# Matmuls of the identity behind the first sums and scores, and the sums' second half moved behind the first scores

## The chip, the cores and the metric

The kernel runs on one core of a Trainium2 chip. The metric is device time in microseconds of one execution. A core has TensorE (PE in the profile; PEld is its loading of weights), VectorE (DVE), ScalarE (ACT), GpSimd (POOL) and SyncE (SP, which here issues the DMAs).

## What is computed

Three layers over 4 sequences of 576 positions. The change lies in the first, attention with 8 heads of 64 per sequence, so 32 heads, handled as 16 pairs:

```python
def _attn_ref(q, k, v, s) -> np.ndarray:
    B, H, S, D = q.shape
    scale = 1.0 / np.sqrt(D)
    scores = scale * np.matmul(q, k.transpose(0, 1, 3, 2))
    causal = np.triu(np.ones((S, S), dtype=bool), k=1)
    s_pos = np.maximum(s, 0.0)
    cum = np.cumsum(s_pos, axis=-1)
    bias = -(cum[:, :, :, None] - cum[:, :, None, :])
    scores = np.where(causal, -1000000000.0, scores + np.minimum(bias, 0.0))
    scores = scores - np.max(scores, axis=-1, keepdims=True)
    attn = np.exp(scores)
    attn = attn / (np.sum(attn, axis=-1, keepdims=True) + 1e-09)
    return np.matmul(attn, v).astype(np.float32)
```

Behind it come a gated feed-forward layer with a mixing over positions, and a layer that mixes positions with weights turned by the sine and cosine of a projection.

## The kernel before

Values in 32 bits are multiplied as a high and a low part, three matmuls for one product. The order of an engine's instructions is worked out ahead of the run by a scheduler with a timeline of its own, from priorities and data dependences; `issue_after(x)` puts an instruction behind x on its engine, and `high_priority` puts it ahead of what else is ready. On the chip each engine works through its list in that order.

**The start.** `run` (L899) makes the identity on GpSimd, loads s, and loads Q and K of pair 0 (`load_pair`, L261). `cumulate` (L183) then makes the running sums of s for all 32 heads: 12 matmuls against triangles of ones into two tiles `cumo` (32 rows), copied to `ch` on ScalarE and to `cpos` on VectorE, with `cl` the rest; `cpos` goes to DRAM (`cd`), from where `load_cum` (L272) fetches the sums of later pairs, spread over 128 rows, by DMA. For pair 0 the spread is done by 8 matmuls with a selecting matrix `sel` into two tiles `cumb`, copied to `C` by ScalarE (L231). `split_pair` (L289) makes qh, ql, kh and kl of a pair on ScalarE, GpSimd and VectorE. Q and K have one buffer each, so a load of K waits for the split kl of the pair before; the four parts and E have two buffers.

**The scores.** `score_units` (L305) works in two groups per pair, for both heads at once on the two halves of the array's rows: the first has tiles t = 4, 1 and 0, the second t = 3 and 2. Each product is three pairs of matmuls, and the causal mask is added by pairs of bf16 matmuls (`mpick`, `mlow`). All matmuls of a group are put one behind the other by `row` (L108) into one tile `sc` of four PSUM banks, of which there is one. VectorE then adds C and takes the extremum of each row (L344), which frees the tile for the next group; ScalarE takes the exponential (L350).

**The step.** `attention` (L461) goes through 17 steps by the string `ORDER`: in step p come the two score groups of pair p ("s"), the transposes of pair p-1 ("t", `transpose_units` L357, with ScalarE or VectorE copying each bank to `Ef` or `E0`), the product with v of pair p-2 ("v", `pv_units`), the loads and splits of pair p+1 ("p") and conversions of the feed-forward weights ("c", `convert`, whose pieces `PLAN` deals out). Some transposes use the pool `psT` of two banks, and in the first four pairs others use `psF`. From step 5 on the feed-forward layer's matmuls are dealt in between as filling; the first steps have none.

**PSUM** has eight banks. `psS` (the scores, four) and `psT` (two) lie on the right, `psF` (two) on the left; the four banks of `cumulate` lie on the left and are given back before `psF` is made.

Of the kernel before, what the change touches and what calls it, by code (L numbers as in the profile page):

```python
# [9 lines left out]
F32 = mybir.dt.float32  # L10
F32R = mybir.dt.float32r
U32 = mybir.dt.uint32
BF16 = mybir.dt.bfloat16
# [3 lines left out]
PSUM = bass.MemoryType.PSUM  # L17
DRAM = bass.MemoryType.DRAM

B, H, S, D = 4, 8, 576, 64  # L20
DM, DFF = 512, 1024
FH = DFF // 2
P = 128
# [14 lines left out]
HALF = [(0, 288), (288, 288)]  # L38
# [15 lines left out]
class Kernel:  # L54
# [50 lines left out]
    def mm(self, out, lhsT, rhs, start, stop):  # L105
        return self.nc.tensor.matmul(out, lhsT, rhs, start=start, stop=stop)  # L106

    def row(self, calls):  # L108


        before = None
        for c in calls:
            with ExitStack() as es:
                if before is not None:
                    es.enter_context(self.tc.high_priority())
                    es.enter_context(self.tc.issue_after(before.ins))
                before = self.mm(*c)


    def pace(self, ns):  # L120
# [62 lines left out]
    def cumulate(self, es):  # L183
        nc = self.nc
        p, sT = self.cum, self.sT
        ps = self.pool(es, "cumps", space=PSUM)
        self.cpos = cpos = p.tile([32, S], F32, name="cpos")


        tri = p.tile([P, 832], F32R, name="tri")  # L190
        neg = p.tile([P, 544], F32R, name="neg")
        sh = p.tile([P, 5, 32], F32R, name="sh")
        sl = p.tile([P, 5, 32], F32R, name="sl")
        trif = p.tile([P, P], F32, name="trif")
        nc.gpsimd.memset(trif, 1.0)
        nc.gpsimd.affine_select(
            out=trif, in_=trif, pattern=[[1, P]], compare_op=ALU.is_ge, fill=0.0, base=0, channel_multiplier=-1
        )
        nc.vector.memset(f32(tri[:, 0:512]), 0.0)
        nc.vector.memset(f32(tri[:, 512 + P:]), 1.0)  # L200
        nc.vector.tensor_copy(tri[:, 512:512 + P], trif)
        nc.vector.memset(f32(neg[:, 0:256]), -1.0)
        nc.vector.memset(f32(neg[:, 256 + P:]), 0.0)
        nc.vector.tensor_scalar(neg[:, 256:256 + P], trif, -1.0, None, op0=ALU.add)
        nc.vector.tensor_scalar(sT, sT, 0.0, None, op0=ALU.max)
        nc.vector.tensor_copy(sh, sT)
        nc.vector.tensor_tensor(sl, sT, f32(sh), op=ALU.subtract)
        ch = p.tile([32, S], F32R, name="ch")
        cl = p.tile([32, S], F32R, name="cl")
        sel = p.tile([32, 2, P], F32R, name="sel")  # L210
        nc.vector.tensor_copy(sel, self.ident[0:32, 0:2].unsqueeze(2).to_broadcast([32, 2, P]))
        self.cums[0] = self.a1.tile([P, 2, S], F32, name="C", tag="C", bufs=2)
        for a, n in HALF:
            o = ps.tile([P, 512], F32, name="cumo", tag=f"cumo{a}")
            tiles = ((0, neg, 256), (1, neg, 128), (2, tri, 256)) if a == 0 else (
                (2, tri, 544), (3, tri, 416), (4, tri, 288))
            for i, (t, w, c) in enumerate(tiles):
                for part in (sh, sl):
                    self.mm(o[0:32, 0:n], part[:, t, :], w[:, c:c + n],
                            i == 0 and part is sh, i == 2 and part is sl)  # L220
            cs = slice(a, a + n)
            nc.scalar.copy(ch[:, cs], o[0:32, 0:n])
            nc.vector.tensor_copy(cpos[:, cs], o[0:32, 0:n])
            nc.sync.dma_start(self.cd[:, cs], cpos[:, cs])
            nc.vector.tensor_tensor(cl[:, cs], cpos[:, cs], f32(ch[:, cs]), op=ALU.subtract)

            for j in (0, 1):
                o = ps.tile([P, 512], F32, name="cumb", tag="cumb", bufs=2)
                self.mm(o[:, 0:n], sel[:, j], ch[:, cs], True, False)
                self.mm(o[:, 0:n], sel[:, j], cl[:, cs], False, True)  # L230
                nc.scalar.copy(self.cums[0][:, j, cs], o[:, 0:n])  # L231

    def attention_pools(self, es):
        nc = self.nc
# [20 lines left out]
            self.nc.vector.memset(r, 0.0)  # L255

    def attention_psum(self, es):
        self.psS = self.pool(es, "psS", side="right", space=PSUM)
        self.psT = self.pool(es, "psT", bufs=2, side="right", space=PSUM)

    def load_pair(self, pr):  # L261
# [43 lines left out]
    def score_units(self, pr):  # L305

        nc = self.nc
        qh, ql, kh, kl = self.ops.pop(pr)
        C = self.cums.pop(pr)
# [5 lines left out]
        for group in GROUPS:  # L315
            calls, sums, cost = [], [], 0.0
            four = self.psS.tile([P, 2, 2, 512], F32, name="sc", tag="sc")
            for i, bank in enumerate(group):
                o = four[:, i]
                for t, a, n, col in bank:  # L320
# [13 lines left out]
                    if a == 0:  # L334
                        sums.append((t, four[:, :, :, 0:n] if t == 4 else four[:, i:i + 1, :, col:col + n]))
                    cost += 3 * max(107.0, w / 2.4) + 120 * len(masks) + 120
            self.row(calls)
            for t, o in sums:
                c = (t - 1) % 5
                n = QE[t]  # L340
# [120 lines left out]
    def attention(self):  # L461
        n = B * H // 2
        for p in range(n + 1):
            su = self.score_units(p) if p < n else iter(())
            tu = self.transpose_units(p - 1) if p > 0 else iter(())

            v = p > 1 and (p - 2) % 4 != 3
            pv = self.pv_units(p - 2) if v else iter(())
            for o in self.ORDER_V if v else self.ORDER:
                if o == "r":  # L470
                    if p > 0:
                        self.load_r(p - 1)
                    continue
                if o == "c":
                    self.convert(p)
                    continue
                if o == "p":
                    if p + 1 < n:
                        self.load_cum(p + 1)
                        self.split_pair(p + 1)  # L480
                    if p + 2 < n:
                        self.load_pair(p + 2)
                    if p < n - 1:
                        with self.tc.issue_after(self.summed[p + 1].ins):
                            self.load_v(p)
                    elif p < n:
                        self.load_v(p)
                    continue
                c = next({"s": su, "t": tu, "v": pv}[o], None)
                self.mark()  # L490
                if c is not None:
                    self.pace(c)
            self.run_units([tu])
            if p > 0 and p % 4 == 0:
                self.run_units([self.pv_units(p - 1)])
                b = p // 4 - 1
                if b < B - 1:
                    self.drain()
                    self.fill = self.ffn(b)
# [399 lines left out]
    def run(self):  # L899
        nc = self.nc  # L900
        with ExitStack() as root, ExitStack() as right2, ExitStack() as left2:
# [9 lines left out]
            self.ident = self.cp.tile([P, P], F32, name="ident")  # L911
            make_identity(nc, self.ident)
            self.attention_pools(att)
            self.load_s(cs)
            self.load_pair(0)
            with self.tc.high_priority():
# [2 lines left out]
            self.load_pair(1)  # L919
            self.constants()  # L920
            self.fill_aux()
            cs.close()
            self.f1 = self.pool(left, "f1")
            self.f2 = self.pool(left, "f2", bufs=2)
# [1 line left out]
            self.f3 = self.pool(f3s, "f3")  # L926
            self.in_done, self.ratio = True, self.RATIO_IN
            self.ffn_weights()
            psl = ExitStack()
            self.psF = self.pool(psl, "psF", bufs=2, side="left", space=PSUM)  # L930
            self.ftags, self.turn = ("fo",), 0
            with ExitStack() as aps:
                self.attention_psum(aps)
                self.attention()
            att.close()
# [131 lines left out]
```

## Time and profile before

| What | Value |
|---|---|
| Median of 3 runs | 674.57 us (673.63 to 678.18) |
| Profiled execution | 674.18 us, of which the span is 672.3 us |
| TensorE busy | 634.8 us, 94% of the span, 4676 matmuls |
| Weight loads (PEld) | 556.9 us, 83% |
| VectorE busy | 427.4 us, 64% |
| ScalarE busy | 363.2 us, 54% |
| GpSimd busy | 179.0 us, 27% |
| DMA | 83.57 MB, mean 124 GB/s |
| TensorE, 0 to 80 us | 65.19 of 80 us |
| TensorE, 80 to 420 us | 320.94 of 340 us |

A share of busy time is a mean over stages with different limits; the stage that the change touches is the first 60 us or so. Matmuls of one engine are pipelined, so the printed durations of neighbours overlap, and the distance between two starts is the better measure of what one costs. The granted clock is given as a share of full speed: 1.00 is 2.4 GHz, 0.50 is 1.2 GHz, and a value between the two means a change of level inside the stretch.

### The profile page before, as it was taken

How to read it: one execution, taken by the hardware profiler on the slowest of the kernel's cores; microseconds unless marked ns; L12 is line 12 of the kernel's file. 1: busy time of each engine (PE TensorE's matmuls, PEld its weight loads, DVE VectorE, ACT ScalarE, POOL GpSimd, SP SyncE). 2: the span in 40 equal slices, each digit the busy share in tenths (PEclk: the TensorE clock that was granted, in tenths of full speed). 3: DMA queues.
4: the chain of work that ended last, by engine and by line, in shares of the span. 5: the costliest groups of instructions: out<-in, count | busy, mean ns of one | idle time of the engine just before them, and what ended most of it. 6: DMA issues, size and time to landing. Idle time of an engine off the chain costs nothing.

```text
span 672.3 us, 12581 instructions
## 1 busy us (share of the span) xinstructions
PE 634.8 (94%) x4676; PEld 556.9 (83%) x4676; DVE 427.4 (64%) x1048; ACT 363.2 (54%) x836; POOL 179.0 (27%) x203
## 2 busy tenths in 40 slices
PE   5889989989999999999997888999999999999997
PEld 4666667778777888778787788898999999989997
DVE  5578856765567563773259977887773477458412
ACT  3767768774688844775155435565550454245100
POOL 4234532433314423044397633220000100100000
PEclk9989999999999999999999889999999999999999
DMA  4556753266632565201355879831001200300101
GB/s 145 190 182 215 233 163 120 77 191 207 203 104 74 169 190 185 73 31 63 119 144 162 266 244 356 264 109 61 1 1 70 73 0 36 106 1 1 71 1 71
DMA packets 50189, 83.57 MB, mean 124 GB/s; under 512 B 8432, under 2 KB 20176, under 8 KB 50128
## 3 DMA queue, kind: packets, MB, share of 16 engines
q1 hardware_dynamic: 50128, 82.76, 38.4%
q8 instruction: 37, 0.61, 0.4%
q14 instruction: 24, 0.20, 0.1%
HBM read 61.61 MB, written 21.13 MB: 123 GB/s over the span
## 4 chain that ended last, share of the span: by engine, by line
PE 65%; ACT 10%; DMA 8%; DVE 8%; POOL 4%; issue 4%; SPq 1%; DVEq 0%; ACTq 0%; POOLq 0%
PE yo L106 17%; PE fo L106 13%; PE th L106 8%; PE co L106 8%; PE wo L106 6%; PE Y L106 4%; PE sc L106 4%; PE T L375 4%; ACT E L350 3%; POOL vT L653 2%; DMA wraw<-in_moe_w_tok_i 1%; PE tp L802 1%; DMA wraw<-in_moe_w_tok_r 1%; DMA wraw<-wd 1%; ACT vT L701 1%
## 5 line engine op out<-in xcount | busy, mean ns | idle before, releaser
L350 ACT ACTIVATE E<-E,negm 128x576 f32<-128x576 f32 (+4 forms) x160 | 92.8, 587 | 2.3 <-DVE negm L344 2.1
L106 PE MATMUL yo<-wkh,zh 128*128 128x288 f32 x288 | 85.3, 296 | 0.2 <-DVE x2T L875 0.2
L106 PE MATMUL yo<-wkl,zh 128*128 128x288 f32 x288 | 85.2, 296 | 0.0
L106 PE MATMUL yo<-wkh,zl 128*128 128x288 f32 x288 | 85.2, 297 | 0.0
L344 DVE CUSTOM_DVE_ANT_0 E<-sc,C 128x576 f32<-128x576 f32 (+4 forms) x160 | 68.2, 486 | 13.5 <-PE sc L106 11.3
L375 PE MATMUL T<-ident,E 128*128 128x128 f32 x400 | 64.2, 292 | 11.1 <-ACT Ef L383 5.6
L375 PEld LDWEIGHTS T<-ident,E 128*128 128x128 f32 x400 | 54.0, 193 | 17.1 <-ACT Ef L383 8.8
L106 PE MATMUL fo<-x,wih 128*128 128x288 f32 x256 | 56.0, 304 | 1.4 <-ACT uT L721 1.4
L106 PEld LDWEIGHTS yo<-wkh,zh 128*128 128x128 f32 x288 | 54.1, 188 | 0.7 <-DVE x2T L875 0.4
L106 PEld LDWEIGHTS yo<-wkl,zh 128*128 128x128 f32 x288 | 54.1, 188 | 0.3
L106 PEld LDWEIGHTS yo<-wkh,zl 128*128 128x128 f32 x288 | 54.0, 188 | 0.1
L106 PE MATMUL co<-u,wch 128*128 128x288 f32 x256 | 53.0, 295 | 0.0
L99 POOL TENSOR_SCALAR xt<-x2s 128x128 fp32r<-128x128 f32 x16 | 10.8, 688 | 155.8 <-DVE x2s L103 155.8
L106 PE MATMUL wo<-gh,woh 128*128 128x288 f32 x128 | 39.3, 310 | 8.1 <-ACT gh L95 4.7
L106 PEld LDWEIGHTS fo<-x,wih 128*128 128x128 f32 x256 | 41.8, 188 | 4.0 <-ACT uT L721 2.2
L106 PE MATMUL fo<-wih,x 128*128 128x512 f32 x128 | 43.3, 404 | 1.3 <-ACT x L95 0.7
L387 DVE COPY Ef<-T 128x512 f32<-128x512 f32 x32 | 21.8, 684 | 34.9 <-PE T L375 31.5
L106 PE MATMUL th<-wth,x2s 128*128 128x512 f32 x128 | 42.9, 400 | 0.0
L95 ACT CAST u<-x2T 128x576 fp32r<-128x576 f32 x16 | 10.7, 672 | 59.3 <-DVE x2T L875 59.3
L106 PE MATMUL sc<-kl,qh 64*128 64x288 f32 (+1 forms) x192 | 39.0, 397 | 3.0 <-DVE negm L344 3.0
L106 PEld LDWEIGHTS co<-u,wch 128*128 128x128 f32 x256 | 41.7, 188 | 0.0
L297 POOL TENSOR_TENSOR kl<-K,kh 128x576 fp32r<-128x576 f32 x15 | 21.8, 1452 | 67.2 <-ACT kh L95 36.9
(193 smaller groups left out, 1775.7 us busy)
## 6 DMA issues: line engine op xcount, KB each, us to landing
C<-cd SPq DMA_DIRECT2D x15, 576.0 KB, 6.1
Q<-in_q SPq DMA_DIRECT2D x16, 288.0 KB, 3.8
K<-in_k SPq DMA_DIRECT2D x16, 288.0 KB, 3.9
xT<-rd SPq DMA_DIRECT2D x32, 144.0 KB, 2.9
xd<-xT SPq DMA_DIRECT2D x16, 288.0 KB
gd<-uT SPq DMA_DIRECT2D x16, 288.0 KB, 4.4
gr<-gd SPq DMA_DIRECT2D x16, 288.0 KB
xr<-xd SPq DMA_DIRECT2D x16, 288.0 KB, 3.5
```

What stands on the lines that cost most here:

```text
L95: nc.scalar.copy(out, src)
L99: nc.gpsimd.tensor_scalar(out, src, 1.0, 1.0, op0=ALU.mult, op1=ALU.mult)
L106: return self.nc.tensor.matmul(out, lhsT, rhs, start=start, stop=stop)
L297: low = nc.gpsimd.tensor_tensor(kl, K, f32(kh), op=ALU.subtract)
L344: nc.vector.tensor_tensor_reduce(at.rearrange("p (i n) -> p i n", i=m), o[:, :, j], C[:, j, 0:n].rearrange("p (i n) -> p i n", i=m), -1.0, ...
L350: nc.scalar.activation(at, at, AF.Exp, bias=negm[:, j, c:c + 1], scale=-1.0, accum_out=sm[:, j * 5 + c:j * 5 + c + 1])
L375: nc.tensor.transpose(T[:, col:col + P], e, self.ident)
L387: nc.vector.tensor_copy(Ef[:, 512:1024], T)
L653: nc.gpsimd.tensor_scalar(vT[0:r, t], vT[0:r, t], rs[0:r, t:t + 1], nm[0:r, t:t + 1], op0=ALU.mult, op1=ALU.add)
L701: nc.scalar.activation(vT, vT, AF.Gelu_apprx_tanh)
L802: nc.tensor.transpose(tp[0:r, dt * P:(dt + 1) * P], x2T[:, dt, a:a + r], self.ident)
```

## The change

A new method `spin` issues n matmuls of the identity, read as 256 columns of bf16, into a PSUM tile that nothing reads. Each is put behind the one before it, at high priority. There are spins at three kinds of places: 14 at the head of `cumulate`; 20 behind the sums' second half in pair 0, into a tile `spun` that takes a bank of `cumo`; and 12 behind the second score group of pairs 0, 1 and 2, into a bank of `psT`.

The 8 matmuls that spread the first pair's sums, and their ScalarE copies, become a function `spread`, which `score_units` calls for pair 0 behind the last matmul of the first score group. For that, the first group of pair 0 is generated before `cumulate`'s pools are given back, `psS` is opened ahead of `cumulate`, and `attention` takes up the generator that has been started. `row` now returns its last matmul.

```diff
--- before.py
+++ after.py
@@ -105,6 +105,18 @@
     def mm(self, out, lhsT, rhs, start, stop):
         return self.nc.tensor.matmul(out, lhsT, rhs, start=start, stop=stop)
 
+    def spin(self, o, n, before=None):
+
+
+        one = self.ident.bitcast(BF16)
+        for _ in range(n):
+            with ExitStack() as es:
+                if before is not None:
+                    es.enter_context(self.tc.issue_after(before.ins))
+                    es.enter_context(self.tc.high_priority())
+                before = self.mm(o[:, 0:256], one[:, 0:P], one, True, True)
+        return before
+
     def row(self, calls):
 
 
@@ -115,6 +127,7 @@
                     es.enter_context(self.tc.high_priority())
                     es.enter_context(self.tc.issue_after(before.ins))
                 before = self.mm(*c)
+        return before
 
 
     def pace(self, ns):
@@ -185,6 +198,23 @@
         p, sT = self.cum, self.sT
         ps = self.pool(es, "cumps", space=PSUM)
         self.cpos = cpos = p.tile([32, S], F32, name="cpos")
+        o = ps.tile([P, 512], F32, name="spin", tag="cumb", bufs=2)
+        self.spin(o, 14)
+        self.spun = ps.tile([P, 512], F32, name="spun", tag="cumo0")
+
+        def spread(before):
+
+            for a, n in HALF:
+                cs = slice(a, a + n)
+                for j in (0, 1):
+                    o = ps.tile([P, 512], F32, name="cumb", tag="cumb", bufs=2)
+                    with self.tc.issue_after(before.ins):
+                        self.mm(o[:, 0:n], sel[:, j], ch[:, cs], True, False)
+                        last = self.mm(o[:, 0:n], sel[:, j], cl[:, cs], False, True)
+                    nc.scalar.copy(C[:, j, cs], o[:, 0:n])
+            return last
+
+        self.spread = spread
 
 
         tri = p.tile([P, 832], F32R, name="tri")
@@ -209,7 +239,7 @@
         cl = p.tile([32, S], F32R, name="cl")
         sel = p.tile([32, 2, P], F32R, name="sel")
         nc.vector.tensor_copy(sel, self.ident[0:32, 0:2].unsqueeze(2).to_broadcast([32, 2, P]))
-        self.cums[0] = self.a1.tile([P, 2, S], F32, name="C", tag="C", bufs=2)
+        C = self.cums[0] = self.a1.tile([P, 2, S], F32, name="C", tag="C", bufs=2)
         for a, n in HALF:
             o = ps.tile([P, 512], F32, name="cumo", tag=f"cumo{a}")
             tiles = ((0, neg, 256), (1, neg, 128), (2, tri, 256)) if a == 0 else (
@@ -224,12 +254,6 @@
             nc.sync.dma_start(self.cd[:, cs], cpos[:, cs])
             nc.vector.tensor_tensor(cl[:, cs], cpos[:, cs], f32(ch[:, cs]), op=ALU.subtract)
 
-            for j in (0, 1):
-                o = ps.tile([P, 512], F32, name="cumb", tag="cumb", bufs=2)
-                self.mm(o[:, 0:n], sel[:, j], ch[:, cs], True, False)
-                self.mm(o[:, 0:n], sel[:, j], cl[:, cs], False, True)
-                nc.scalar.copy(self.cums[0][:, j, cs], o[:, 0:n])
-
     def attention_pools(self, es):
         nc = self.nc
         side = "right"
@@ -255,7 +279,6 @@
             self.nc.vector.memset(r, 0.0)
 
     def attention_psum(self, es):
-        self.psS = self.pool(es, "psS", side="right", space=PSUM)
         self.psT = self.pool(es, "psT", bufs=2, side="right", space=PSUM)
 
     def load_pair(self, pr):
@@ -334,7 +357,11 @@
                     if a == 0:
                         sums.append((t, four[:, :, :, 0:n] if t == 4 else four[:, i:i + 1, :, col:col + n]))
                     cost += 3 * max(107.0, w / 2.4) + 120 * len(masks) + 120
-            self.row(calls)
+            last = self.row(calls)
+            if pr < 3 and group is GROUPS[-1]:
+                self.spin(self.psT.tile([P, 512], F32, name="spin", tag="T"), 12, last)
+            elif pr == 0:
+                self.spin(self.spun, 20, self.spread(last))
             for t, o in sums:
                 c = (t - 1) % 5
                 n = QE[t]
@@ -461,7 +488,7 @@
     def attention(self):
         n = B * H // 2
         for p in range(n + 1):
-            su = self.score_units(p) if p < n else iter(())
+            su = self.first if p == 0 else self.score_units(p) if p < n else iter(())
             tu = self.transpose_units(p - 1) if p > 0 else iter(())
 
             v = p > 1 and (p - 2) % 4 != 3
@@ -486,7 +513,10 @@
                     elif p < n:
                         self.load_v(p)
                     continue
-                c = next({"s": su, "t": tu, "v": pv}[o], None)
+                if p == 0 and o == "s" and self.lead:
+                    c, self.lead = self.lead, None
+                else:
+                    c = next({"s": su, "t": tu, "v": pv}[o], None)
                 self.mark()
                 if c is not None:
                     self.pace(c)
@@ -911,6 +941,9 @@
             self.ident = self.cp.tile([P, P], F32, name="ident")
             make_identity(nc, self.ident)
             self.attention_pools(att)
+            psl = ExitStack()
+            aps = ExitStack()
+            self.psS = self.pool(aps, "psS", side="right", space=PSUM)
             self.load_s(cs)
             self.load_pair(0)
             with self.tc.high_priority():
@@ -919,6 +952,8 @@
             self.load_pair(1)
             self.constants()
             self.fill_aux()
+            self.first = self.score_units(0)
+            self.lead = next(self.first)
             cs.close()
             self.f1 = self.pool(left, "f1")
             self.f2 = self.pool(left, "f2", bufs=2)
@@ -926,10 +961,9 @@
             self.f3 = self.pool(f3s, "f3")
             self.in_done, self.ratio = True, self.RATIO_IN
             self.ffn_weights()
-            psl = ExitStack()
             self.psF = self.pool(psl, "psF", bufs=2, side="left", space=PSUM)
             self.ftags, self.turn = ("fo",), 0
-            with ExitStack() as aps:
+            with aps:
                 self.attention_psum(aps)
                 self.attention()
             att.close()
```

## Rows read from the trace of the kernel before

**Rows 1.** Busy by stretch: PE, PEld, DVE, ACT, POOL; clock, DMA share, GB/s.

```profile
0.00:80.00 80.00, 65.19 (x515) 48.45 (x517) 55.70 (x173) 52.76 (x152) 32.05 (x43) 0.94 0.59 184
80.00:420.00 340.00, 320.94 (x2448) 271.31 (x2445) 219.40 (x593) 207.90 (x507) 134.70 (x144) 0.99 0.50 159
```

**Rows 2.** TensorE's timeline, pair 0: start us, us, what, count, [idle, releaser].

```profile
4.30 0.45 PE L106 MATMUL cumo<-neg,sh 128*32 128x288 f32 x1 [4.30 <-DVE sh L206]
...
7.18 0.44 PE L106 MATMUL cumo<-tri,sl 128*32 128x288 f32 x1
...
8.73 0.44 PE L106 MATMUL sc<-kh,ql 64*128 64x288 f32 x2
8.97 0.44 PE L106 MATMUL sc<-kh,qh 64*128 64x288 f32 x2
...
9.80 0.44 PE L106 MATMUL sc<-mpick,mlow 64*128 64x128 bf16 x4
10.00 0.59 PE L106 MATMUL sc<-kl,qh 64*128 64x288 f32 x2
...
13.99 0.44 PE L106 MATMUL cumb<-cl,sel 32*128 32x288 f32 x1
```

**Rows 3.** TensorE's timeline, pairs 1, 2 and 4.

```profile
21.96 0.61 PE L106 MATMUL sc<-kl,qh 64*128 64x288 f32 x2
...
25.38 0.33 PE L106 MATMUL sc<-mpick,mlow 64*128 64x128 bf16 x2
...
28.10 0.47 PE L106 MATMUL sc<-kl,qh 64*128 64x448 f32 x2 [0.17 <-DVE negm L344]
...
29.44 0.29 PE L106 MATMUL sc<-mpick,mlow 64*128 64x128 bf16 x4
...
32.79 0.70 PE L375 MATMUL T<-ident,E 128*128 128x128 f32 x2 [1.24 <-ACT E L350]
33.42 0.61 PE L106 MATMUL sc<-kl,qh 64*128 64x288 f32 x2
...
47.15 0.49 PE L375 MATMUL T<-ident,E 128*128 128x128 f32 x1 [2.44 <-ACT Ef L383]
...
63.19 0.40 PE L106 MATMUL sc<-kl,qh 64*128 64x288 f32 x2
...
65.05 0.23 PE L106 MATMUL sc<-mpick,mlow 64*128 64x128 bf16 x2
```

**Rows 4.** Busy in half microseconds, columns as in rows 1.

```profile
32.50:33.00 0.50, 0.21 (x1) 0.21 (x2) 0.00 (x0) 0.50 (x3) 0.50 (x1) 0.93 0.78 281
...
36.00:36.50 0.50, 0.50 (x12) 0.50 (x10) 0.00 (x0) 0.00 (x0) 0.00 (x0) 0.66 0.89 370
46.50:47.00 0.50, 0.00 (x0) 0.00 (x0) 0.50 (x3) 0.50 (x3) 0.50 (x1) 0.58 0.07 8
```

**Rows 5.** Chain of waits, in order of time: start us, us, what.

```profile
7.81 3.14 DMA K<-in_k
...
13.79 0.76 DVE ql L300
...
16.90 2.89 PE sc L106 x20
...
22.30 3.44 DMA C<-cd
...
32.05 0.70 ACT E L350 x2
...
33.49 3.35 PE sc L106 x27
...
44.18 1.79 DVE wtab L510
...
51.91 0.74 DVE E L344
```

**Rows 6.** GpSimd's timeline: the identity.

```profile
2.16 0.30 POOL masks.py:199 TENSOR_SCALAR_AFFINE_SELECT ident<-ident 128x128 f32<-128x128 f32 x1
```

## The prediction

> **What bounds the kernel now.** I read the busy time by stretch first [rows 1]. From 80 us on, TensorE is busy 320.94 of 340 us, so 94%: there the order of TensorE's work sets the time, and the change adds nothing to it. In the first 80 us it is busy 65.19 us, so some 15 us are waits. A microsecond won there reaches the end, because everything later starts that much sooner; a microsecond won on TensorE where another engine is late is lost again.
>
> The second view is TensorE's timeline of the first pair of heads [rows 2]. The two matmuls of a score pair run side by side, and pairs of 288 columns start 0.24 us apart (8.73, 8.97): 288 / 0.24 = 1.2 columns per ns, the lower of the clock's levels, 1.2 GHz. That stands although the clock column prints 0.94 as the mean of the first 80 us; the reader is to go by the starts here. The same groups later show the other level [rows 3]: the first score group of a pair takes 21.96 to 25.38 + 0.33 = 25.71, 3.75 us, in pair 1, and 63.19 to 65.05 + 0.23 = 65.28, 2.09 us, in pair 4. The second group takes 2.89 us from 16.90 in pair 0 [rows 5] and 28.10 to 29.44 + 0.29 = 29.73, 1.63 us, in pair 1. The prices of the low level are thus 3.75 - 2.09 = 1.66 us for a first group and 2.89 - 1.63 = 1.26 us for a second.
>
> Third, the granted clock in half microseconds [rows 4], where it is recorded. 0.93 at 32.5 to 33.0 means a fall to half; it comes in the wait that ends at 32.79 [rows 3]. 0.66 at 36.0 to 36.5 is the rise, behind the scores that run from 33.42. 0.58 at 46.5 to 47.0 is the next fall, in the wait of 2.44 us that ends at 47.15. So pair 2 begins its scores at the low level as pairs 0 and 1 do, and pair 3 may.
>
> Last, the chain of waits [rows 5]: it shows which of these groups matter. Until 14.5 us the end is set by the loads and splits of K (K for pair 1 is asked for at 7.81, its last split is DVE's ql at 13.79) and not by TensorE. From 16.90 on, score groups and DVE's reductions alternate, since one score tile is all there is. Around 43 us DVE's weight conversions enter.
>
> **The change part by part.** The sum is made against the profiled execution, 674.18 us (span 672.3, the rest lies around it); the median of the runs is 0.39 us above that.
>
> (a) 14 spins stand ahead of the sums. The identity is ready at 2.16 + 0.30 = 2.46 [rows 6]. The trace shows no spin; the nearest rows are the bf16 mask matmuls, of which four, two side by side, fill 9.80 to 10.00, 0.10 us for 128 columns [rows 2], so 256 columns cost about 0.21 us at the low level and 0.11 at the high one. 14 x 0.21 = 3.0 us, to 5.5: the first sum moves from 4.30 to 5.5 and the twelfth ends near 8.8 instead of 7.62 [rows 2]. I cost this at nothing: the scores of pair 0 start some 0.2 us later, the sums' copies are ready near 14 us (an estimate: the first group's 3.7 us, then about 2 us for the eight matmuls of the spread), and DVE's first reduction starts at 14.55 behind ql anyway [rows 5]. If that cover were gone, it would be 1.2 us.
>
> (b) The spread of the sums. Before, part of these eight matmuls came ahead of the scores and the rest, to 13.99 + 0.44, behind them [rows 2]. Now all eight come behind; ScalarE's copies still precede 14.5. Nothing, between -0.3 and +0.3.
>
> (c) 20 spins behind the spread. TensorE works through its queue in order, so they hold whatever stands behind them, which is the second score group of pair 0, and DVE and the exponentials wait for that. From 14.2 on they cost 4.3 us at the low level (to 18.5, 1.6 us past the 16.90 at which that group started) and 2.2 us at the high one (to 16.4, nothing). The nearest row is the rise near the end of the scores from 33.42 [rows 4], so I choose a value nearer to the low level: spins to 18.0, +1.1, between 0 and +1.6.
>
> (d) The second group of pair 0 at the high level: -1.26, or 0 if the clock has not risen. With (c) its end moves from 16.90 + 2.89 = 19.79 to about 19.63.
>
> (e) 12 spins behind it: 1.3 us at the high level, in the time in which DVE reduces that group and TensorE had waited for ScalarE: nothing. At the low level 2.6 us, +0.5.
>
> (f) The first group of pair 1, at 21.96 before: -1.66, or 0. The chain has a load of C there, 22.30 to 25.74 [rows 5]; but the scores ended at 25.71, and by the code the load issued in step 1 is that of pair 2, which this reduction doesn't read, so I put it down to the scores.
>
> (g) 12 spins behind pair 1's second group. The rest of pair 0's transposes stood behind it, and ScalarE copies those ahead of the exponentials (32.05) that release the transposes at 32.79 [rows 3, 5]. +0.5, between 0 and +1.3.
>
> (h) The spins fill most of the gaps up to 32.79, so the clock need not fall, and the first group of pair 2 (33.42 [rows 3] to 33.49 + 3.35 = 36.84 [rows 5], 3.42 us) takes 2.09: -1.33, or 0.
>
> (i) 12 spins in pair 2's wait of 2.44 us: hidden, and the clock need not fall there [rows 3, 4]. But the first group of pair 3 has to be reduced by DVE, which is held by conversions (1.79 us for one at 44.18) and reaches it at 51.91 [rows 5]. -0.4 of a possible -1.66.
>
> Sum: 1.1 - 1.26 - 1.66 + 0.5 - 1.33 - 0.4 = -3.05. 674.18 - 3.05 = 671.1; counted from the median it is 671.5, and I take 671.3.
>
> The trace shows a blocked queue at 32.79: two transposes wait 1.24 us for an exponential and pair 2's scores stand behind them [rows 3]. The Trainium skill (TensorE: Matmul & The Clock Gate, Part 2, the step on LDWEIGHTS) says the same of the engine in general: only weight loads are pulled ahead, matmuls stay in program order. By that rule alone, every spin still running when real work is ready is a loss, and the sum would be +1.1 + 0.5 = +1.6 (675.8); by the rows of the clock the shorter groups more than pay for it. The Trainium skill (TensorE: Matmul & The Clock Gate, Part 1, What's actually happening) puts the whole penalty of a cold start below 1% of a typical kernel's span. By it the change could not give 6.7 us; the rows' groups at the low level, with the first pair's own, come to somewhat more (the second rival), and I keep a chance for that.
>
> **The rivals.** (1) The spins raise the clock no sooner than before, or too late. For: matmuls filled most of 4.30 to 14.4 us, and the group at 16.90 still took 2.89 us [rows 2, 5]. Against: pair 2's scores did raise it within one group [rows 4]. Then c, e and g cost 1.6 + 0.5 + 0.5, d and f give nothing, h stays: +1.3, 675.5. (2) The clock rises during the first spins and stays. Then pair 0's first group takes 2.1 instead of 3.7 us, its sums are copied by 12, and, if DVE's order then has the reduction ahead of ql, it starts up to 2.4 us sooner; c and g vanish: with 1.0 for pair 3, -2.4 - 1.26 - 1.66 - 1.33 - 1.0 = -7.65, 666.5. Against it: the K chain up to 13.79 is untouched [rows 5]. (3) Slower: in steps 1 and 2 the spins take one of only two banks that the transposes use, so they wait for a ScalarE copy that stands behind exponentials, and the whole queue waits with them. The longest such wait is 2.44 us [rows 3]; two of them, with only the gain of the first pair and pair 1 (-1.8) left, make +3.1, 677.3. It decides from 1.5 us per wait on. (4) It makes no difference, because DVE's conversions around 44 us [rows 5] take back what is won: 674.
>
> **How the numbers follow.** Forecast 0.50, rival (1) 0.15, (2) 0.17, (3) 0.12, (4) 0.06. The likeliest gives 671.3, its own range 669 to 674. 667 to 677 leaves out half of (2) and half of (3). Faster by over 1% (below 667.8) is most of (2), 0.15; slower by over 1% (above 681.3) needs (3) in all three steps, 0.04; within 1%, about what a measurement of this kernel can tell from no change, 0.81.
>
> **What would show it.** Right: pairs of 288 columns 0.14 us or less apart in pair 1's first group, the second group of pair 0 starting near 18, no fall of the granted clock up to 55 us, and DVE's first reduction still near 14.5. Wrong: a granted clock of 0.5 in pair 2's first group, spins that wait for a ScalarE copy, or a first reduction well ahead of 14 us.

## The result and the profile after

The changed kernel takes 667.11 us (666.18 to 669.12), the kernel before 676.25 us (673.63 to 679.69) beside it: the ratio is 0.987 (0.985 to 0.989), some 9 us. The profiled execution takes 667.05 us with a span of 665.3 us, 7.0 us less than the span of before; the two medians lie further apart than the two profiles, because the profiled execution of before, 674.18 us, lies near the low end of its runs.

The page of the profile after, its first part and the clock's row (tenths, 40 slices):

```profile
span 665.3 us, 12716 instructions
...
PE 631.6 (95%) x4746; PEld 555.3 (83%) x4746; DVE 426.8 (64%) x1048; ACT 364.1 (55%) x836; POOL 181.9 (27%) x203
...
PEclk9998999999999999999999989999999999999999
```

Busy time by stretch after, columns as in [rows 1]:

```profile
0.00:80.00 80.00, 68.40 (x622) 51.90 (x624) 61.54 (x192) 57.16 (x166) 35.01 (x44) 0.98 0.66 207
80.00:420.00 340.00, 321.55 (x2451) 272.30 (x2450) 218.84 (x589) 208.52 (x502) 137.52 (x148) 0.99 0.51 160
...
5.00:6.00 1.00, 1.00 (x7) 0.69 (x5) 0.08 (x1) 0.20 (x1) 0.68 (x1) 1.00 0.08 30
```

TensorE lost 3.2 us of busy time, although 70 more matmuls are recorded (70 are added), so the work that is left ran faster; and 65.19 us in the first 80 became 68.40, since later work moved forward. TensorE's timeline after, from the spins at the head to the fourth pair's second score group (start us, duration us, line, operands, count, [idle before, releaser]; `spun` are the 20):

```profile
2.07 3.17 PE L106 MATMUL spin<-ident 128*128 128x256 bf16 x14 [2.07 <-POOL ident masks.py:199]
...
5.28 0.44 PE L106 MATMUL cumo<-tri,sh 128*32 128x288 f32 x1
5.52 0.44 PE L106 MATMUL cumo<-neg,sl 128*32 128x288 f32 x1
...
8.26 0.30 PE L106 MATMUL sc<-kh,ql 64*128 64x288 f32 x2
8.39 0.29 PE L106 MATMUL sc<-kh,qh 64*128 64x288 f32 x2
...
13.07 2.36 PE L106 MATMUL spun<-ident 128*128 128x256 bf16 x20
17.22 0.47 PE L106 MATMUL sc<-kl,qh 64*128 64x448 f32 x2 [1.79 <-DVE negm L371]
...
18.53 0.31 PE L106 MATMUL sc<-mpick,mlow 64*128 64x128 bf16 x4
...
21.03 0.40 PE L106 MATMUL sc<-kl,qh 64*128 64x288 f32 x2 [0.65 <-POOL kl L320]
...
22.85 0.27 PE L106 MATMUL sc<-mpick,mlow 64*128 64x128 bf16 x2
...
27.16 1.48 PE L106 MATMUL spin<-ident 128*128 128x256 bf16 x12
...
28.82 0.60 PE L402 MATMUL T<-ident,E 128*128 128x128 f32 x4
29.41 0.40 PE L106 MATMUL sc<-kl,qh 64*128 64x288 f32 x2
...
34.90 0.47 PE L106 MATMUL sc<-kl,qh 64*128 64x448 f32 x2 [0.94 <-DVE negm L371]
...
38.66 1.08 PE L106 MATMUL Y<-E,v 128*64 128x512 f32 x4
```

The reader is to see four things. The sums from 5.28 to 5.52 still start 0.24 us apart, so the clock is low, and by 8.26 pairs of 288 columns start 0.13 us apart (8.26, 8.39): it rose near 7.5 us, at the sums, and not during the 20 spins, as I had chosen in (c). The second group of pair 0 starts at 17.22, not earlier than before (16.90), and takes 1.62 us (to 18.53 + 0.31). Pair 1's first group takes 2.09 us (21.03 to 22.85 + 0.27). And then, which I had not seen at all: pair 2's second score group (34.90) comes *ahead* of the product Y (38.66). Before, Y came first.

TensorE's timeline before, at the same place:

```profile
38.40 1.08 PE L106 MATMUL Y<-E,v 128*64 128x512 f32 x4
...
41.68 0.47 PE L106 MATMUL sc<-kl,qh 64*128 64x448 f32 x2
```

VectorE's first reduction after (start us, duration us):

```profile
14.11 0.76 DVE L323 SCALAR_TENSOR_TENSOR ql<-Q,qh 128x576 fp32r<-128x576 f32 x1 [4.73 <-POOL qh L322]
14.79 0.75 DVE L371 CUSTOM_DVE_ANT_0 E<-sc,C 128x576 f32<-128x576 f32 x1
```

Here is how far the second score group of a pair moved from the kernel before, in the profiles (worked out from the starts of the first matmul of 448 columns in each):

| | pair 0 | 1 | 2 | 3 | 4 | 6 | 8 | 15 | end |
|---|---|---|---|---|---|---|---|---|---|
| before, start us | 16.9 | 28.1 | 41.7 | 57.4 | 71.0 | 108.0 | 148.1 | 299.0 | 672.3 |
| after | +0.3 | -2.5 | -6.8 | -9.1 | -9.4 | -9.0 | -6.5 | -6.3 | -7.0 |
| no 12s | -0.2 | -3.1 | -4.9 | -4.0 | -3.0 | -3.6 | -0.3 | -0.6 | -1.8 |
| Y behind, no spins | +0.1 | -1.6 | -5.6 | -8.8 | -8.4 | -7.8 | -5.8 | -5.7 | -5.6 |
| narrow spins | +0.1 | +1.0 | -3.2 | -5.4 | -5.0 | -4.5 | -2.3 | -2.1 | -2.5 |

The rows behind the first two belong to the experiments below. A start tells what is won only where TensorE has issued the same work by then. In the kernels with Y behind, 20 matmuls of Y (3.2 us) are still to come at pairs 2 to 4, and at pair 6 they have issued 12 matmuls of the feed-forward layer and 3 transposes fewer than the kernel before; at pair 1 the kernels with the 12s have issued 7 transposes fewer. At pairs 5, 7 and 8 the counts are those of before, apart from the spins, and there the same profiles read:

| | pair 5 | 7 | 8 | end |
|---|---|---|---|---|
| before, start us | 84.5 | 127.8 | 148.1 | 672.3 |
| after | -5.3 | -5.3 | -6.5 | -7.0 |
| after, a second profile | -2.6 | -4.2 | -5.9 | -7.2 |
| no 12s | -3.1 | -3.6 | -0.3 | -1.8 |
| Y behind, no spins | -4.1 | -4.1 | -5.8 | -5.6 |
| narrow spins | +0.7 | -0.8 | -2.3 | -2.5 |

So the -9.4 at pair 4 is not a lead that is later lost: of it, 3.2 us are Y put off, and with equal work the change is 5.3 us ahead at pair 5 and 7.0 at the end. Part of the lead arises only between pairs 7 and 8.

### The profile page after: what moved, and what is told of

Its sections match the earlier page's. It is cut to its first block, busy times and chain, and to the rows that moved or that the text cites. A ratio compares the mean times of both kernels' runs of the same rounds, so it can differ in the third digit from the quotient of the medians.

```text
span 665.3 us, 12716 instructions
## 1 busy us (share of the span) xinstructions
PE 631.6 (95%) x4746; PEld 555.3 (83%) x4746; DVE 426.8 (64%) x1048; ACT 364.1 (55%) x836; POOL 181.9 (27%) x203
## 4 chain that ended last, share of the span: by engine, by line
PE 66%; DVE 9%; ACT 9%; POOL 6%; DMA 5%; issue 3%; SPq 1%; DVEq 0%; POOLq 0%; ACTq 0%
PE yo L106 17%; PE fo L106 13%; PE th L106 8%; PE co L106 8%; PE wo L106 6%; PE sc L106 5%; PE Y L106 4%; PE T L402 4%; ACT E L377 3%; POOL vT L683 2%; DVE E L371 2%; PE tp L832 1%; DMA gr<-gd 1%; ACT vT L731 1%; DMA K<-in_k 1%
## 5 line engine op out<-in xcount | busy, mean ns | idle before, releaser
L402 PE MATMUL T<-ident,E 128*128 128x128 f32 x400 | 62.7, 291 | 6.6 <-DVE xT L460 4.1
L106 PE MATMUL sc<-kl,qh 64*128 64x288 f32 (+1 forms) x192 | 36.1, 366 | 4.8 <-DVE negm L371 4.2
```

The source lines that it names most:

```text
L402: nc.tensor.transpose(T[:, col:col + P], e, self.ident)
```

## The experiments

Theory A says that the clock makes the gain, as the prediction had it; theory B, formed on this profile, says that the order of the engines' work does, above all the place of Y. Ratios are to the kernel before on the same chip, with their 95% interval.

| Kernel | Y in steps 2 to 4 | Spins | Time, us | Ratio |
|---|---|---|---|---|
| the change | behind the second group | 14, 20, 12s | 667.1 | 0.9869 (0.9847 to 0.9891) |
| spread alone | ahead | none | 675.8 | 1.000 (0.9985 to 1.0015) |
| without the 12s | ahead | 14, 20 | 674.6 | 0.998 (0.996 to 1.000) |
| Y put ahead | ahead | 14, 20, 12s | 674.9 | 0.997 (0.996 to 0.998) |
| Y put behind, kernel before | behind | none | 670.4 | 0.991 (0.988 to 0.995) |
| without the 12s, Y put behind | behind | 14, 20 | 668.2 | 0.988 (0.983 to 0.992) |
| narrow spins | behind | of 32 rows | 671.6 | 0.9935 (0.992 to 0.995) |
| without the 14 | behind | 20, 12s | 669.4 | 0.990 (0.988 to 0.992) |

**The spread alone.** The 8 matmuls move, and no spin is there:

```diff
-        o = ps.tile([P, 512], F32, name="spin", tag="cumb", bufs=2)
-        self.spin(o, 14)
...
-                self.spin(self.psT.tile([P, 512], F32, name="spin", tag="T"), 12, last)
...
-                self.spin(self.spun, 20, self.spread(last))
+                self.spread(last)
```

> The eight matmuls of the spread are moved behind the first scores, and there are no spins. Theory A: no gain, 673 to 677, with score groups of pairs 0 to 2 at the low level (3.75 and 2.9 us). Theory B: another order alone can win or lose several us, so 668 to 672, or above 678.

675.75 us, ratio 1.000. The move by itself is worth nothing, and a new order is not a gain by itself either: the groups stand where they stood, within 0.4 us down to pair 7.

**Without the 12s.**

```diff
-            if pr < 3 and group is GROUPS[-1]:
-                self.spin(self.psT.tile([P, 512], F32, name="spin", tag="T"), 12, last)
-            elif pr == 0:
+            if pr == 0 and group is GROUPS[0]:
                 self.spin(self.spun, 20, self.spread(last))
```

> Without the 12 spins behind the second groups of pairs 0, 1 and 2; the 14 and the 20 stay. Theory A: the clock rises near 7.5 us, falls again in one of the waits of steps 0 to 3, and a group or two run at the low level: 1.3 to 3.5 us more than with them, 668 to 671. Rival: those spins are in the way as often as they help: 665 to 667.

674.6 us, ratio 0.998: nearly all of the gain is gone, far more than the clock of a group or two, so neither number fits. The first two pairs are as fast as with the 12s (table above: -3.1 at pair 1). What changes is step 2: without the 12s, Y stands ahead of pair 2's second group again. Why the 12s bring the other order was not tried apart; by the code they take a bank of `psT`, of which Y and its last part Z need both, so the scheduler can't place these two before the spins are done.

The chain of waits shows where the 3.6 us that were still there at pair 7 went:

```profile
134.63 6.46 DMA gt<-in_moe_w_sg
...
141.12 0.43 ACT wsrh L95
141.55 0.49 ACT Ef L408
...
142.09 0.91 PE T L400 x3
```

A piece of a weight that took 4.45 us to load in the kernel before takes 6.46 us here, and ScalarE's conversion of it stands in front of the copy that TensorE's transposes wait for. The kernel before has this chain too:

```profile
138.34 4.45 DMA gt<-in_moe_w_sg
...
142.82 0.43 ACT wsrh L95
143.25 0.49 ACT Ef L383
...
143.79 0.62 PE T L375 x3
```

The load is asked for 3.7 us sooner (134.63 against 138.34) and lands only 1.7 us sooner. TensorE waits 3.99 us ahead of the transposes at 142.09 (1.66 us before), and behind that wait the clock is low:

```profile
142.00:144.00 2.00, 1.91 (x10) 1.89 (x10) 1.06 (x3) 0.52 (x3) 0.79 (x1) 0.50 0.37 110
```

In the changed kernel the last two pieces are asked for from 129.37 on, and this wait is not there:

```profile
129.37 1.12 SPq L626 DMA_DIRECT2D gt<-in_moe_w_sg  x2
...
132.66 0.43 ACT L95 CAST wsrh<-gt 128x288 fp32r<-128x288 f32 x1
```

The profiles part the same way throughout: in the four kernels with Y ahead (before, the spread alone, without the 12s, Y put ahead) TensorE waits 1.3 to 4.0 us near 143 us, and in none of those with Y behind does it wait longer than 1.2 us for a ScalarE copy between 130 and 146 us.

**The order alone.** In the kernel before, Y is put behind the second score group for the first three pairs, and nothing else in the program is changed:

```diff
...
-        self.row(calls)
+        with ExitStack() as es:
+            if pr < 3:
+                es.enter_context(self.tc.issue_after(self.scored.ins))
+            self.row(calls)
```

(`scored` is the last matmul of the group scored last.)

> The kernel before, without spins and without the moved spread; only the product with v of the first three pairs is put behind the second score group of its step, which is where the changed kernel has it. Theory B (the order makes about half of the gain): 669.5 to 672.5, with pairs 0 to 2 at the low level as before. Theory A (the clock makes all of it): 674 to 677.

670.43 us, ratio 0.991 (0.988 to 0.995): 5.9 of the 9 us, without one spin. TensorE's timeline:

```profile
22.05 0.41 PE L106 MATMUL sc<-kl,qh 64*128 64x288 f32 x2
...
23.88 0.27 PE L106 MATMUL sc<-mpick,mlow 64*128 64x128 bf16 x2
...
36.11 0.47 PE L106 MATMUL sc<-kl,qh 64*128 64x448 f32 x2 [0.85 <-DVE negm L345]
...
37.67 1.08 PE L106 MATMUL Y<-E,v 128*64 128x512 f32 x4
38.58 2.32 PE L106 MATMUL Y<-Ef,vr 128*64 128x512 f32 x16
```

The first reduction of pair 2's second group no longer waits for the 3.2 us of Y (38.40 to 41.68 before), and ScalarE and VectorE get their next work by that much sooner. One caution: in this profile pair 1's first group ran at the high level (22.05 to 23.88 + 0.27, 2.10 us) and the clock stood at 1.00 from there on to 40 us, whereas it took 3.75 us in the profile of before; up to there the two kernels issue the same work on TensorE, so the profile flatters the order by the 1.7 us at pair 1, and perhaps by 1.3 more at pair 2's. It is the fastest of the four executions (668.47; the others 670.33 to 670.56), and the median doesn't hang on it.

The edit also does more than move Y. From 38 us on the scheduler orders the work of the other engines anew, and of this profile's 5.6 us, 1.7 come between pairs 7 and 8, where the wait for the weight is gone. How much each part gives was not tried apart: what is shown is the worth of the order that comes with Y behind.

**The order in place of the 12s.** The kernel without the 12s, with the same edit:

> The changed kernel without the 12s, but with the product with v put behind the second score group by hand in steps 2 to 4. Theory B: the 12s worked mainly by the order that they brought, so 666.5 to 669 here against 674.6 without it. Theory A: the 12s worked by keeping the clock up in steps 2 and 3, so 671 to 675.

668.2 us, ratio 0.988 (0.983 to 0.992), against 0.998 without the edit: the 12s worked mainly by the order that they brought, though pair 2's first group took 3.5 us in this profile (30.4 to 33.9), so the clock did fall without them. The other way round, all spins with the old place of Y:

```diff
-            for o in self.ORDER_V if v else self.ORDER:
+            for o in "scttvsptcrttctc" if v and p < 5 else self.ORDER_V if v else self.ORDER:
...
-            last = self.row(calls)
+            with ExitStack() as es:
+                if 1 < pr < 5 and group is GROUPS[-1]:
+                    es.enter_context(self.tc.issue_after(self.summed_y.ins))
+                last = self.row(calls)
```

(`summed_y` is the last matmul of Z.)

> The changed kernel with all its spins, but with the product with v put ahead of the second score group in steps 2 to 4, as the kernel before has it. If the order makes about two thirds of the gain: 672 to 675. If the clock makes it: 667 to 669.

674.85 us, ratio 0.997 (0.996 to 0.998). That is not quite the order of before: VectorE waits twice for a load of xT, 4.8 us between 20 and 60 us, which it did not do there. With the kernel without the 12s (0.998), which has no such wait, it says the same: on the old order the spins give 0.2 to 0.3% of the whole (the two intervals reach from 0 to 0.44%). In both profiles what they had won by pair 7 (3.6 and 0.7 us) is lost at pair 8, behind the wait for the weight (3.99 and 3.42 us).

**The same order with a lower clock.** The spins take 32 rows of the identity, in the same places; of TensorE's instructions only a handful around step 3 stand otherwise than in the changed kernel.

```diff
-                before = self.mm(o[:, 0:256], one[:, 0:P], one, True, True)
+                before = self.mm(o[:, 0:256], one[0:32, 0:P], one[0:32], True, True)
```

> The spins take 32 rows of the identity instead of 128; columns, places and all but a few entries of the engines' order stay those of the changed kernel. Theory A (the clock): the gain is the clock's, and it rises because of what the spins feed the array. If narrow spins don't raise it, pair 1's first score group takes about 3.75 us again and the time is 674 to 677; if they do, 667. Theory B (the order): the scheduler's new order of steps 1 to 4 makes most of the gain, for instance pair 2's second score group ahead of the product with v. Then the time is 667 to 671 even with groups of 3.75 us.

671.6 us, ratio 0.9935 (0.992 to 0.995), between the two theories. TensorE's timeline, from the spread to pair 1's first group, and the clock behind 14 us:

```profile
11.53 0.29 PE L106 MATMUL cumb<-ch,sel 32*128 32x288 f32 x1
11.66 0.29 PE L106 MATMUL cumb<-cl,sel 32*128 32x288 f32 x1
...
19.75 2.73 PE L106 MATMUL spin<-ident 32*128 32x256 bf16 x12
...
22.84 0.61 PE L106 MATMUL sc<-kl,qh 64*128 64x288 f32 x2
...
26.26 0.33 PE L106 MATMUL sc<-mpick,mlow 64*128 64x128 bf16 x2
```

```profile
14.00:15.00 1.00, 1.00 (x6) 0.71 (x5) 1.00 (x2) 0.00 (x0) 0.40 (x1) 0.50 0.66 118
```

The clock rose with narrow spins too, near 10.3 us (sums of 288 columns start 0.13 us apart at 11.53), fell near 13.7, and stood at 0.50 from there to 27.4 us. Pair 1's first group takes 22.84 to 26.59, 3.75 us, as before, and the 12 spins ahead of it take 2.73 us and start it 0.9 us late. So with the order, and a low clock from pair 0's second group to pair 1's first, the kernel keeps about half of the gain, and pays for the spins in the queue besides.

**Without the 14.**

```diff
-        o = ps.tile([P, 512], F32, name="spin", tag="cumb", bufs=2)
-        self.spin(o, 14)
```

> Without the 14 spins at the head; the 20 and the 12s stay. Theory A as predicted (the first reduction is held to 14.8 us by the loads and splits of K): the clock rises during the 20 spins or shortly behind them, pair 0's second group starts between 16.9 and 18.5, and the time is 667 to 669. Rival: the head's spins are what raises the clock for all that follows; without them the 20 run at the low level, the second group starts near 18.5 and takes 2.9 us, and the time is 670 to 673.

669.4 us, ratio 0.990 (0.988 to 0.992), 0.4 us above what theory A expected and 0.6 below what the rival did. The 20 spins ran partly at the low level (3.9 us, 12.8 to 16.7) and ended just before pair 0's second group, which took 1.61 us from 16.92. Pairs 1 to 4 stand where they do with the 14, so in the profile the difference arises later; that the 14 give 2 us by the clock is not shown.

**The change once more.**

> The changed kernel unchanged, on the chip of the three others, as their measure: ratio 0.985 to 0.989 to the kernel before, 666 to 669 us. Its profile is a second look at where the clock rises and falls: by theory A up from near 7.5 us to the wait near 56 us in this one too; if the moment of the rise moves from run to run, it differs by some us.

667.6 us, ratio 0.986 (0.984 to 0.988). Its profile differs from the first one just where the prediction put the gain:

```profile
13.00:14.00 1.00, 1.00 (x11) 0.88 (x9) 0.19 (x1) 0.28 (x1) 0.94 (x3) 0.96 0.00 0
14.00:15.00 1.00, 1.00 (x7) 0.72 (x5) 1.00 (x2) 0.00 (x0) 0.36 (x1) 0.50 0.71 136
...
20.00:21.00 1.00, 1.00 (x8) 0.71 (x7) 1.00 (x5) 0.81 (x2) 0.56 (x1) 0.62 0.38 139
```

```profile
12.78 3.38 PE L106 MATMUL spun<-ident 128*128 128x256 bf16 x20
16.91 0.74 PE L106 MATMUL sc<-kl,qh 64*128 64x448 f32 x2 [0.75 <-DVE negm L371]
...
19.32 0.46 PE L106 MATMUL sc<-mpick,mlow 64*128 64x128 bf16 x4
```

The clock had risen near 7 us and fell again near 14, during the 20 spins, which stand behind a wait of 1.39 us for the copies of the sums. The second group of pair 0 took 16.91 to 19.32 + 0.46, 2.87 us, as before. The time is the same within 0.5 us, although this execution is 2.7 us behind the first profile at pair 5: at pair 7 it is 1.1 us behind, and at the end 0.2 us ahead.

**More spins.** 12 also behind the second groups of pairs 3 and 4.

```diff
-            if pr < 3 and group is GROUPS[-1]:
+            if pr < 5 and group is GROUPS[-1]:
```

> The changed kernel, with 12 spins also behind the second groups of pairs 3 and 4. They fill the wait near 56 us, so the fall of the clock near 58 us should go, and with it up to 2 us of transposes at the low level: 665 to 667. Rival: DVE holds steps 4 and 5, or the spins turn the order of those steps for the worse: 667 to 670.

670.2 us, ratio 0.991 (0.988 to 0.993): 3 us slower than the change by the medians, though the intervals just touch. The order turned again: Y of step 3 moved behind pair 4's first group, whose matmuls wait 1.79 us, and pair 4's second group starts at 65.55 instead of 61.68.

```profile
53.87 0.40 PE L106 MATMUL sc<-kl,qh 64*128 64x288 f32 x2 [1.79 <-DVE negm L371]
...
56.91 1.63 PE L106 MATMUL Y<-E,v 128*64 128x512 f32 x4
...
65.55 0.47 PE L106 MATMUL sc<-kl,qh 64*128 64x448 f32 x2 [0.87 <-DVE negm L371]
```

**The chain that holds the first reduction.** In the changed kernel, pair 1's Q and K are loaded into a buffer that is still free:

```diff
+        if pr == 1:
+            T = self.a2.tile([P, 1280], F32, name="Ef", tag="Ef", bufs=3)
+            Q, K = T[:, 0:S], T[:, 640:640 + S]
...
```

> The changed kernel, with Q and K of pair 1 loaded into a buffer that is still free, so that they don't wait for the splits of pair 0. If the first reduction was held to 14.8 us by that chain of loads and splits alone, it starts at 11.5 to 13.6 us and the time is 663.5 to 666. If the copies of the spread sums, or a longer load of pair 0's K beside the new ones, hold it then, it stays within 0.5 us of 14.8 and the time at 666 to 668.

664.9 us, ratio 0.984 (0.980 to 0.988). VectorE's first reduction:

```profile
11.11 0.74 DVE L327 SCALAR_TENSOR_TENSOR ql<-Ef,qh 128x576 fp32r<-128x576 f32 x1
12.28 0.76 DVE L375 CUSTOM_DVE_ANT_0 E<-sc,C 128x576 f32<-128x576 f32 x1 [0.43 <-ACT C L214]
```

It starts at 12.28 and now waits for ScalarE's copy C of the sums; in the kernel before it started at 14.47, and in the changed one at 14.79. That it was held by the loads and splits of K is shown. The gain over the change is 2.2 us by the medians, with intervals that overlap.

The same on the kernel before with Y behind, and no spins:

> No spins, the spread as before: the product with v behind the second group (as in the run that gave 670.4) and pair 1's Q and K loaded early (as in the run that gave 664.9). If the two act on different parts, the first reduction starts near 13.9, when the copies of the sums end, and the time is 669 to 670.5, since without spins the sums' copies come late. If the early load gives its 2 us here too: 667.5 to 669.

667.1 us, ratio 0.986 (0.982 to 0.990), below both expectations; the first reduction starts at 11.87, not near 13.9. Two edits without a spin reach what the change reaches. And with the 14 and the 20 spins, Y behind by hand and no 12s:

> The 14 and the 20 spins, the spread, the early load of pair 1, and the product with v behind the second group by hand in place of the 12s. If the 12s gave no more than that order: 664 to 666, as with them. If they also keep the clock up: 666 to 669.

664.2 us, ratio 0.981 (0.979 to 0.984), the fastest, ahead of the changed kernel run beside it (0.986, 0.984 to 0.988). The 14 and the 20 are thus worth 2.9 us beside the run just above, which has none, with intervals that overlap. The 12s are not needed once the order is written down.

## Why the prediction was right or wrong

The direction was right. The range, 667 to 677, held 667.11 by a tenth of a microsecond, and that is luck: 3 us were forecast and 9 found, I had given 0.15 to more than 1%, and two thirds of the gain come from something that the sum doesn't have.

**The step that failed is (i) with its neighbour (g): the steps beyond pair 1, and the order in them.** I priced the 12s as matmuls in a fixed order, +0.5 in step 1 and -0.4 for step 3. They changed the order: Y went behind the second group in steps 2 to 4. That term is missing from the sum, and the order with Y behind measured -5.9 us by itself (ratio 0.991). The chain that I read holds a part of it, with 33.49 PE sc and 44.18 DVE wtab [rows 5] and, between the two, Y:

```profile
38.47 3.21 PE Y L106 x20
```

I read it as work to be done and not as work in the way of a group that VectorE waits for. The other part lies where I looked for nothing: of the stretch from 80 us on I wrote that the change adds nothing to it, but there the order takes away the wait for the weight near 143 us.

**The clock's terms, (c) to (f) and (h)**, were sized rightly where the clock was up: 1.62 us for pair 0's second group (I had 1.63), 2.09 for the first groups of pairs 1 and 2. Their sum is -3.2 without the 12s' terms. On the order that I assumed, the profile without the 12s is ahead by about that much at pair 1 (3.1 us) and at pair 7 (3.6 us), and then loses it; of the whole, the spins gave 0.2 to 0.3% there (1.3 to 2.0 us). On the new order they give 2.2 us (670.4 without spins, 668.2 with the 14 and 20) or 2.9 (667.1 and 664.2, with pair 1 loaded early); all of them, the 12s too, give 0.4% (0.991 and 0.987) or 0.2% (0.986 and 0.984, with pair 1 loaded early). The intervals overlap each time. So the size was about right, and what failed is that it would reach the end on the old order. Two things were not as assumed. The groups of before do not stand at the low level in every execution: with the same work up to there, pair 1's first group took 3.75 us in one profile and 2.10 us in another. And the second group of pair 0 may run at the low level in the changed kernel without a loss to the whole.

**(a) and (b)** were right: the identity is made first now, at 1.72 us on GpSimd, the spins run from 2.07, and the sums end near 8.0, not 8.8; nothing came of it, as the first reduction is held by K. It starts at 14.79 after ql (14.11), as the prediction said it would, and the early load shows why. (c) cost nothing and not +1.1, since the clock had risen before the 20, which end at 13.07 + 2.36 = 15.43: TensorE then waits 1.79 us for VectorE, and the group starts 0.3 us later than before only because the first reduction does.

**The wait at 32.79** [rows 3] is gone: pair 2's first group starts at 29.41 behind seven transposes that wait for nothing. That is an order too, but not Y's: with Y put behind by hand and without the 12s, the wait of 1.25 us is still there, with and without the 14 and 20.

**"A microsecond won there reaches the end"** did not hold in general. Without the 12s, 3.6 us won by pair 7 are 0.3 at pair 8, where a weight's load stands in front of ScalarE's copies. In the changed kernel 2.7 us lost by pair 5 in the second profile don't show at the end.

**The rivals.** (2) has the nearest time (666.5) and the early rise, but not its mechanism: the first reduction did not come sooner. (1) is refuted by the spins at the head, (3) did not come in this change, though the spins behind pairs 3 and 4 did turn the order for the worse. (4) describes the old order best, where the spins come to almost nothing (0.998), but it is a weight's load near 140 us that takes the gain, not VectorE's conversions around 44. The rule of the Trainium skill that matmuls stay in program order (TensorE: Matmul & The Clock Gate, Part 2) bore more than I took from it: it is Y ahead of the scores that costs, and with narrow spins the queue's delay is seen, 0.9 us at pair 1. The rule that a cold start costs less than 1% (the same page of the Trainium skill, Part 1) agrees with the runs: the spins give 0.2 to 0.3% of the whole on the old order and 0.2 to 0.5% on the new one, and the larger part of the gain is the order's.

## What to carry to other kernels

Before a filler or any small edit is costed, ask which buffer it holds and how the scheduler's order turns around it: here 12 matmuls that nothing reads, in one of two banks, moved a product of 3.2 us out of the way of the group that all other engines wait for, with the later loads and copies moved as well, and that order was worth more than the clock. Before two profiles are compared by the start of a group, count whether the same work has been issued by then. If a gain appears, write the order that made it down by itself and take the filler away. And where a first stage is held by a chain of loads and splits, a free buffer for the next load can be worth as much as the faster engine (2.2 us here).

## What the runs showed of the hardware

The moments at which the clock rises and falls move from execution to execution. The kernel before and the one with Y behind issue the same matmuls up to pair 1's first group; the first rise that their profiles record is at 26.1 and at 20.4 us, and that group took 3.75 and 2.10 us. Two more profiles without spins have it at 9.5 us (the spread alone) and 7.3 us (Y behind and pair 1 loaded early). In all eight profiles with the 14 spins of 128 rows it comes between 5.2 and 7.7 us. In six of these the clock fell again between 12 and 14 us, and in two, the first of the changed kernel among them, it stayed up past 55 us. So the 14 go with an early rise; they did not keep the clock up. The changed kernel's two profiles differ by some 7 us at the low level (13.9 to 20.8 us). That the count of slow matmuls at the start varies from run to run is also what the Trainium skill says (TensorE: Matmul & The Clock Gate, Part 1, What's actually happening); the traces agree, with these numbers.

With spins of 32 rows the rise came at 10.3 us and a fall at 13.7; with no spins at all (the spread alone) 9.5 and 12.9. From one profile of each, nothing can be said of what the rows of the spins do.

A lower mean clock is not always a longer time. Of the 19 executions of the kernel before on one chip, the 11 with a mean granted clock of 0.985 or more have a median of 676.07 us, and the four with 0.977 or less 676.12. In the ten without the 12s the time does go with the clock, from 679.22 us at 0.971 to 672.18 at 0.987.

The clock column prints 1.00 for the stretch ahead of the first event (5 to 6 us in the profile of the change, where the sums of 288 columns start 0.24 us apart): there the starts of matmuls tell the level, not the column.
